# Gate vectors and norm columns of a fused adaLN, attention and gMLP kernel: from fp32 sums to float32r sums, with the columns by way of memory

## The chip, the cores and the metric

The kernel runs on one core of a Trainium2 chip. The time is that of one execution on the device, in microseconds; a result is the median of three timed runs. A profile is one further execution with the hardware profiler on. In the profile PE is the matrix engine (PEld its weight loads), DVE the vector engine, ACT the scalar engine, POOL is GpSimd, and SP issues most DMAs. Each engine works through a queue of its own in order; the engines wait for each other by semaphores.

## What is computed

The input is x (2048 tokens of 448 numbers) with a conditioning vector c. From c come six vectors of 448: `sa`, `ca`, `ga` for the attention block and `sb`, `cb`, `gb` for the second block.

```
mod = silu(c) @ w_mod                      # six vectors: sa, ca, ga, sb, cb, gb
h = layernorm(x) * (1 + ca) + sa
x = x + ga * (attention(h @ wqkv, 16 heads of 28) @ wo)
h = layernorm(x) * (1 + cb) + sb
z = gelu(h @ w_in);  z1 = z[:, :896];  z2 = layernorm(z[:, 896:])
x = x + gb * ((z1 * (w_sp @ z2 + b_sp)) @ w_out)
```

`sa, ca, sb, cb` are needed as columns (one number a partition), because they scale the transposed tokens. `ga` and `gb` are needed as rows repeated in all 128 partitions.

## The kernel before

Nearly every matmul uses float32r operands, which PE takes at full pace but with a shortened mantissa. To keep accuracy each operand is held as a high part (a float32r copy) and a low part (the rest), and the products high by high, high by low and low by high are summed: the list `STEPS` has eleven such products for one tile.

The order on each engine is that of the program's text (`manual_schedule`); the program lays it out by hand. PSUM has a ring of seven banks (`bank`), and one bank beside it. The tokens are worked on in four groups of 512 (`g`), 128 tokens a tile (`t`).

The part that the change touches is the projections, the first 90 us:

- `ln_stat` (DVE) takes mean and variance of a token tile, `ln_rs` (GpSimd) turns the variance into 1/std, `ln_norm` (DVE) writes the normalised tile `xn`, of which ACT copies the last 64 columns once more. `ln_transpose` lets PE transpose sixteen blocks into four banks; ACT scales them (`hfull`) and writes the high part of `hT[g]`, DVE the low part.
- `v_mm`/`v_tile` project V for a tile of tokens; `qk_unit` projects 128 rows of Q and K for a group. Its result is split into `qh` and `ql`, and SP stores both to `qk_scr` in memory, from where `load_head` fetches the rows of one head.
- `qk_part` splits the weights of Q and K: ACT the high part, DVE or GpSimd the low part. Kind "a" is the first 512 columns, in four parts of 128 (the last of 64) rows.
- `mod_acc` (DVE) adds up the products of `silu(c)` with a 112-row slice of `w_mod`; after four slices `acc` holds 112 partial sums for each of two vectors. `mod_bc` (L233) sums over the 112 partitions by one fp32 matmul with a matrix of ones, which gives the row in all partitions; `mod_col` (L228) uses five fp32 matmuls of one column each, and one DVE add. An fp32 matmul stands as two rows in the profile. Pair 0 (`sa`, `ca`) has a path of its own. Pair 1 is (`ga`, `sb`), pair 2 (`cb`, `gb`).

The order in the program: group 0's projections with the weight splits; `ln_next(1)`, which transposes group 1 and takes the statistics of group 2 between the low parts; the Q and K units of group 0; then the loop over g = 1 to 3: two V tiles, `ln_next(g + 1)`, two V tiles with `mod_acc` and, for g = 2, the sums of pair 1 between them, two Q and K units. For g = 3 the first head's tiles `kst` and `qst` are cleared (`pads`), `load_head(0)` and two units come first, then four V tiles and the sums of pair 2. Behind it 18 more units are interleaved with the score matmuls of the first heads (`mt`, L528), and the attention follows.

Tiles come from pools with a fixed number of buffers for a tag. In the pool `stage` the tags `qh` and `qf` have two buffers each; a tile that takes a buffer over waits for the readers of the one before, a DMA among them.

Of the kernel before, what the change touches and what calls it, by code (L numbers as in the profile page):

```python
# [8 lines left out]
F32 = mybir.dt.float32  # L9
F32R = mybir.dt.float32r  # L10
AF = mybir.ActivationFunctionType
ALU = mybir.AluOpType
# [4 lines left out]
S, D, H, DH, FH = 2048, 448, 16, 28, 896  # L17
# [11 lines left out]
STEPS = STEPS_MAIN + STEPS_Z  # L29
# [4 lines left out]
def tile_adaln_mha_gmlp(ctx, tc, x, wqkv, wo, w_in, w_spT, b_sp, w_out, cT, w_mod, out):  # L34
    nc = tc.nc
    ctx.enter_context(tc.manual_schedule())
    pe, dve, act, pool, sp = nc.tensor, nc.vector, nc.scalar, nc.gpsimd, nc.sync
# [3 lines left out]
    scr = ctx.enter_context(tc.tile_pool(name="scr", bufs=1, space=DRAM))  # L41
# [15 lines left out]
    cols = {}  # L57
# [25 lines left out]
    def sub(eng, dst, a, hi):  # L83
        eng.tensor_tensor(out=dst, in0=a, in1=hi.bitcast(F32), op=ALU.subtract)  # L84
# [25 lines left out]
    def ln_transpose(xns, full_pool, dsts, scol, bcol, engs, los=(pool,) * 4, mid=None, after=None):  # L110

        tps = []
        for c in range(4):
            tp = bank("tp")
            tps.append(tp)
            for t in range(4):
                pe.transpose(tp[:, t * 128 : (t + 1) * 128], xns[t][:, c * 128 : (c + 1) * 128], ident)  # L117
        if mid:
            mid()
        for c in (0, 2, 1, 3):  # L120
            tp = tps[c]
            f = full_pool.tile([128, 512], F32, name="hfull")
            if engs[c] is act:
                act.activation(f, tp, AF.Identity, scale=scol[:, c : c + 1], bias=bcol[:, c : c + 1])
            else:
                engs[c].tensor_scalar(
                    out=f, in0=tp, scalar1=scol[:, c : c + 1], scalar2=bcol[:, c : c + 1], op0=ALU.mult, op1=ALU.add
                )
            hi = dsts[:, c if c < 3 else 6, :]
            if engs[c] is act:  # L130
                act.activation(hi, f, AF.Copy)
            else:
                engs[c].tensor_copy(hi, f)
            if c < 3:
                sub(los[c], dsts[:, 3 + c, :], f, hi)
            else:
                sub(los[c], hi[64:128], f[64:128], hi[64:128])
            if after:
                after(c)
# [17 lines left out]
    e2 = late_e.enter_context(tc.tile_pool(name="e2", bufs=1, side="right"))  # L157

    wv = e2.tile([128, 8, D], F32R, name="wv")
    wms, xts, raws = {}, {}, {}  # L160

    def bank(name):
        return ring.tile([128, 512], F32, name=name, tag="s")
# [25 lines left out]
    def qk_part(kind, i, eng):  # L189
        weight_part(wqk, i, raws.pop((kind, i)), act, eng, False, PARTS[kind][0])  # L190
# [26 lines left out]
    accs = {}  # L217

    def mod_acc(pair, k):
        if k == 0:  # L220
            accs[pair] = e2.tile([112, 2, D], F32, name="acc")
        wm, acc = wms.pop((pair, k)), accs[pair]
        if k == 0:
            dve.tensor_scalar(out=acc, in0=wm, scalar1=silu[:, 0:1], scalar2=None, op0=ALU.mult)
        else:
            dve.scalar_tensor_tensor(out=acc, in0=wm, scalar=silu[:, k : k + 1], in1=acc, op0=ALU.mult, op1=ALU.add)

    def mod_col(nm, acc, plus1):  # L228
        pc = bank("pc")
        for c, r, e in ((0, 0, 128), (1, 0, 128), (2, 0, 128), (3, 0, 64), (3, 64, 128)):  # L230
            pe.matmul(pc[r:e, c : c + 1], acc[:, c * 128 : c * 128 + e - r], ones[:112, 0:1], start=True, stop=True)
        dve.tensor_scalar(out=cols[nm], in0=pc[:, 0:4], scalar1=plus1, scalar2=None, op0=ALU.add)

    def mod_bc(nm, acc):
        pc = bank("pc")
        pe.matmul(pc[:, :D], ones[:112, :], acc, start=True, stop=True)
        dve.tensor_copy(bcs[nm], pc[:, :D])

    mv1, xn1 = {}, {}

    def ln_stat(g, ts):
        if g not in mv1:
            mv1[g] = e1.tile([128, 4, 2], F32, name="mv"), e1.tile([128, 4], F32, name="rs")
        for t in ts:
            st = e1.tile([128, 6], F32, name="st", bufs=4)
            dve.bn_stats(out=st, in_=xts[4 * g + t])
            dve.bn_aggr(out=mv1[g][0][:, t, :], in_=st)

    def ln_rs(g, a, e):
        mv, rs = mv1[g]  # L250
        rstd_of(mv[:, a:e, 1], rs[:, a:e], e - a)
# [27 lines left out]
    def v_tile(kt):  # L279
        v_copy(*v_mm((kt,))[0])  # L280

    def qk_unit(ms, g, mid=None):
        pqs = [bank("pq") for _ in ms]
        for j, (a, b) in enumerate(STEPS):
            if mid and j in mid:
                mid[j]()
            for m, pq in zip(ms, pqs):
                pe.matmul(pq, wqk[:, b, m * 128 : (m + 1) * 128], hT[g][:, a, :], start=j == 0, stop=j == NST - 1)  # L288
        for m, pq in zip(ms, pqs):
            hi = stage.tile([128, 512], F32R, name="qh")  # L290
            lo = stage2.tile([128, 512], F32R, name="ql")
            if mid:
                f = stage.tile([128, 512], F32, name="qf")
                act.activation(f, pq, AF.Copy)
                act.activation(hi, f, AF.Copy)
                sub(pool, lo, f, hi)
            else:
                act.activation(hi, pq, AF.Copy)
                sub(dve, lo, pq, hi)
            for i, t in enumerate((hi, lo)):  # L300
                sp.dma_start(qk_scr[i][m * 128 : (m + 1) * 128, g * 512 : (g + 1) * 512], t.bitcast(F32))
# [121 lines left out]
    for i in (0, 2, 1, 3):  # L423
        load_w("b", i, sp)
    pvs = v_mm((0, 1, 3, 2), [STEPS[j] for j in (0, 1, 2, 3, 6, 4, 5, 7, 8, 9, 10)], 3)
    ln_stat(1, (0, 1))
    qk_part("a", 0, dve)
    qk_part("a", 2, dve)
    ln_stat(1, (2, 3))
    ln_rs(1, 0, 4)  # L430
    qk_part("a", 1, dve)
    qk_part("a", 3, dve)
    load_mod(1, sp)
    for a in pvs:
        v_copy(*a)
    ln_norm(1, range(4))
    qk_unit((0, 3), 0)

    def ln_next(g):

        if g + 1 < NG:
            ln_transpose(
                xn1.pop(g), e1, hT[g], cols["ca"], cols["sa"], (act,) * 4, (dve,) * 4, None,
                lambda c: ln_stat(g + 1, ((0, 2, 1, 3).index(c),)),
            )
            ln_rs(g + 1, 0, 4)
            ln_norm(g + 1, range(4))
        else:
            ln_transpose(xn1.pop(g), e1, hT[g], cols["ca"], cols["sa"], (act,) * 4, (dve,) * 4)

    ln_next(1)
    load_x(3, sp)
# [5 lines left out]
    for g in range(1, NG):  # L458
        if g == 3:
            early.close()  # L460
            stk = att.enter_context(tc.tile_pool(name="stk", bufs=1))
            kq = [[stk.tile([128, S], F32R, name=f"{n}st{i}") for n in "kq"] for i in range(3)]
            kst, qst = [a[0] for a in kq], [a[1] for a in kq]
            npool = att.enter_context(tc.tile_pool(name="npool", bufs=2))

            def pads(i, eng):

                dve.memset(kst[i][64:128, :].bitcast(F32), 0.0)
                eng.memset(qst[i][64:128, :].bitcast(F32), 0.0)
                pool.memset(kst[i][64:86, :].bitcast(F32), 1.0)  # L470

            pads(0, dve)

            def load_head(h, c0=0, c1=S):
                k, q = kst[h % 3], qst[h % 3]
                if h > 2:
                    sp.dma_start(q[84:86, :].bitcast(F32), q[86:88, :].bitcast(F32))
                for r0, i in ((0, 0), (56, 1), (28, 0)):
                    sp.dma_start(k[r0 : r0 + 28, c0:c1].bitcast(F32), qk_scr[i][D + h * DH : D + (h + 1) * DH, c0:c1])
                for r0, i in ((0, 0), (28, 1), (56, 0)):  # L480
                    sp.dma_start(q[r0 : r0 + 28, c0:c1].bitcast(F32), qk_scr[i][h * DH : (h + 1) * DH, c0:c1])

            load_head(0, 0, 1536)
            for m in (0, 3):
                qk_unit((m,), g)
            load_head(0, 1536, S)
        v_tile(4 * g)
        v_tile(4 * g + 1)
        if g == 3:
            pads(1, pool)  # L490
            pads(2, pool)
        if g + 1 < NG:
            ln_next(g + 1)
        for k in range(2):
            v_tile(4 * g + 2 + k)
            if g == 2 and k == 0:
                mod_bc("ga", accs[1][:, 0, :])
                mod_col("sb", accs[1][:, 1, :], 0.0)
            if g < 3:
                mod_acc(g, k)  # L500
        if g < 3:
            for k, m in enumerate((0, 3)):
                qk_unit((m,), g)
                mod_acc(g, 2 + k)
    mod_col("cb", accs[2][:, 0, :], 1.0)
    mod_bc("gb", accs[2][:, 1, :])
    late_e.close()


# [579 lines left out]
    acc = {}  # L1089
# [241 lines left out]
```

## Time and profile before

| | |
|---|---|
| median of three runs | 1407.74 us (1406.87 to 1410.05) |
| the profiled execution | 1407.27 us |
| its span, first to last instruction | 1405.3 us |
| granted clock of PE | 1.0 |
| bytes moved by DMA | 186.99 MB, 133 GB/s in the mean |

A row of a timeline gives start, duration (of all instructions merged into it), engine, line, operation, output and inputs, shapes and count; in brackets stands the idle time just before and what ended it. Matmuls are pipelined, so their durations overlap: the pace is read from start to start. A row "SPq" is the issue of a DMA by SP, not its transfer. A row of grouped instructions gives busy time, mean duration in ns, and idle time before.

### The profile page before, as it was taken

Reading aid. Unit: us, or ns where it says so; the run is one execution under the profiler, and the core shown is the slowest. Engines: PE = TensorE matmul, PEld = TensorE weight load, DVE = VectorE, ACT = ScalarE, POOL = GpSimd, SP = SyncE. Lnnn points to the kernel's source line nnn. Section 1 sums busy time; section 2 is a strip of 40 time slices with the busy share of each in tenths; the row PEclk is TensorE's granted clock in tenths of the full one; section 3 lists DMA queues with packets and bytes.
Section 4 is the critical chain, followed back from the end, with each engine's and each line's share of the span. In section 5 each row is a group of like instructions: output and inputs, shape, how many; then the busy total and the mean of one; then the engine's idle time right before and its main releaser. Section 6 shows DMA issues by size and latency. Waiting matters only on the chain.

```text
span 1405.3 us, 20320 instructions
## 1 busy us (share of the span) xinstructions
PE 1394.6 (99%) x7180; PEld 982.8 (70%) x7180; DVE 1011.5 (72%) x1700; ACT 787.6 (56%) x1532; POOL 286.3 (20%) x276
## 2 busy tenths in 40 slices
PE   8999999999999999999999999999999999999998
PEld 7888655555555555555555554988998888888888
DVE  7778888888888888888888860851357555768574
ACT  4623677777777777777777779263234543434211
POOL 3033312222314243313200021100132330001000
PEclk9999999999999999999999999999999999999999
DMA  8564635555455545654423001533103333445453
GB/s 256 156 176 157 190 106 175 167 161 148 162 166 162 160 163 174 180 153 155 127 68 74 22 18 33 192 121 137 55 0 107 111 113 111 144 136 162 142 170 112
DMA packets 98252, 186.99 MB, mean 133 GB/s; under 512 B 16614, under 2 KB 28006, under 8 KB 95606
## 3 DMA queue, kind: packets, MB, share of 16 engines
q1 hardware_dynamic: 95722, 181.87, 42.7%
q10 hardware_dynamic: 2430, 3.84, 0.7%
q8 instruction: 56, 0.92, 0.3%
q14 instruction: 44, 0.36, 0.1%
HBM read 130.42 MB, written 50.45 MB: 129 GB/s over the span
## 4 chain that ended last, share of the span: by engine, by line
PE 95%; DVE 2%; DMA 1%; ACT 0%; issue 0%; POOL 0%; SPq 0%; DVEq 0%; ACTq 0%; POOLq 0%
PE st_ps L559 19%; PE o_ps L574 17%; PE mt L528 17%; PE acc L1099 6%; PE acc L1100 6%; PE acc L1098 6%; PE z_ps L1024 5%; PE z_ps L910 5%; PE pq L288 4%; PE wo_ps L780 3%; PE pv L273 2%; PE y_ps L1203 2%; PE y_ps L1204 2%; PE y_ps L1202 2%; DMA wm<-in_w_mod_dram 1%; PE tp L117 1%
## 5 line engine op out<-in xcount | busy, mean ns | idle before, releaser
L533 DVE TENSOR_REDUCE pm<-mt 128x1 f32<-128x512 f32 x1024 | 631.2, 680 | 108.9 <-PE mt L528 108.8
L563 ACT ACTIVATE P<-st_ps 128x512 f32<-128x512 f32 x1024 | 513.4, 621 | 150.0 <-PE st_ps L559 149.7
L559 PE MATMUL st_ps<-qst,kst 128*128 128x512 f32 x1024 | 407.7, 409 | 0.1
L528 PE MATMUL mt<-kst,qst 128*128 128x512 f32 x1024 | 401.4, 392 | 0.0
L559 PEld LDWEIGHTS st_ps<-qst,kst 128*128 128x128 f32 x1024 | 191.0, 187 | 152.6 <-issue 82.2
L574 PE MATMUL o_ps<-P,V 128*32 128x512 f32 x2048 | 247.5, 598 | 0.0
L528 PEld LDWEIGHTS mt<-kst,qst 128*128 128x128 f32 x1024 | 192.6, 188 | 30.5 <-ACT P L563 0.7
L681 POOL TENSOR_TENSOR ws_raw<-ws_raw 128x512 f32<-128x512 f32 x80 | 103.0, 1287 | 275.6 <-DMA ws_raw<-in_w_spT_dram 275.5
L986 ACT ACTIVATE wsp_h<-raw_sp 128x512 fp32r<-128x512 f32 x112 | 70.0, 631 | 154.2 <-PE acc L1100 102.9
L84 DVE TENSOR_TENSOR wsp_l<-raw_sp,wsp_h 128x512 fp32r<-128x512 f32 x112 | 81.9, 741 | 81.3 <-ACT wsp_h L986 80.6
L574 PEld LDWEIGHTS o_ps<-P,V 128*32 128x32 f32 x2048 | 54.1, 109 | 123.3 <-issue 116.3
L1099 PE MATMUL acc<-wsp_l,heapA 128*128 128x512 f32 x224 | 87.3, 390 | 0.1
L1098 PE MATMUL acc<-wsp_h,heapA 128*128 128x512 f32 x224 | 87.3, 390 | 0.0
L1100 PE MATMUL acc<-wsp_h,heapA 128*128 128x512 f32 x224 | 87.2, 389 | 0.0
L1099 PE MATMUL acc<-wsp_l,heapB 128*128 128x512 f32 x174 | 67.7, 389 | 0.0
L1098 PE MATMUL acc<-wsp_h,heapB 128*128 128x512 f32 x174 | 67.7, 389 | 0.0
L1100 PE MATMUL acc<-wsp_h,heapB 128*128 128x512 f32 x174 | 67.7, 389 | 0.0
L288 PE MATMUL pq<-heapD,heapD 128*128 128x512 f32 x196 | 62.4, 392 | 0.0
L1028 DVE BATCH_NORM_STATS2 stz<-z 128x6 f32<-128x448 f32 x32 | 19.9, 625 | 50.4 <-ACT z L1027 30.1
L1099 PEld LDWEIGHTS acc<-wsp_l,heapA 128*128 128x128 f32 x224 | 42.0, 188 | 9.1 <-DVE wsp_l L84 0.5
L1098 PEld LDWEIGHTS acc<-wsp_h,heapA 128*128 128x128 f32 x224 | 42.0, 188 | 8.9 <-DVE cD L1104 0.3
L1100 PEld LDWEIGHTS acc<-wsp_h,heapA 128*128 128x128 f32 x224 | 42.0, 188 | 8.7
(205 smaller groups left out, 1595.0 us busy)
## 6 DMA issues: line engine op xcount, KB each, us to landing
ws_raw<-in_w_spT_dram SPq DMA_DIRECT2D x160, 256.0 KB
ws_scr<-ws_raw SPq DMA_DIRECT2D x80, 256.0 KB
raw_sp<-ws_scr SPq DMA_DIRECT2D x80, 256.0 KB
kst<-qk_scr SPq DMA_DIRECT2D x45, 224.0 KB
qst<-qk_scr SPq DMA_DIRECT2D x45, 224.0 KB
raw_sp<-in_w_spT_dram SPq DMA_DIRECT2D x32, 256.0 KB
qk_scr<-qh SPq DMA_DIRECT2D x28, 256.0 KB
qk_scr<-ql SPq DMA_DIRECT2D x28, 256.0 KB
```

Source lines behind the costliest of these rows:

```text
L84: eng.tensor_tensor(out=dst, in0=a, in1=hi.bitcast(F32), op=ALU.subtract)
L288: pe.matmul(pq, wqk[:, b, m * 128 : (m + 1) * 128], hT[g][:, a, :], start=j == 0, stop=j == NST - 1)
L528: pe.matmul(mt, qst[h % 3][:, t * 128 : (t + 1) * 128], kst[h % 3][:, kb * 512 : (kb + 1) * 512], start=True, stop=True)
L533: dve.tensor_reduce(out=pms[h][:, t, kb : kb + 1], in_=mt, axis=AX.X, op=ALU.max)
L559: pe.matmul(st, kst[h % 3][:, kt * 128 : (kt + 1) * 128], qst[h % 3][:, qb * 512 : (qb + 1) * 512], start=True, stop=True)
L563: act.activation(p, st, AF.Exp, scale=SCALE)
L574: pe.matmul(otile[h][32 * qb : 32 * qb + 32, :], V[:, kt, h, :], ptiles.pop((u, qb)), start=kt == 0, stop=kt == NT - 1)
L681: pool.tensor_tensor(out=a, in0=a, in1=b, op=SUMS[i // 16][2])
L910: pe.matmul(ps_t, w1[:, b, f * 128 : (f + 1) * 128], h2T[g][:, a, :], start=j == 0, stop=j == NST - 1)
L1098: pe.matmul(acc[i], zh, hi, start=st == 0, stop=False)
L1099: pe.matmul(acc[i], zh, lo, start=False, stop=False)
L1100: pe.matmul(acc[i], zl, hi, start=False, stop=st == 7)
```

## The change

1. Pairs 1 and 2: `mod_split` makes a float32r high part (ACT) and a low part (GpSimd) of each vector's partial sums, in buffers of the tags `qf` and `qh`. `mod_sum` sums both over the partitions by two float32r matmuls with a float32r matrix of ones. `mod_bc` copies the result. `mod_col` takes one partition's row, adds the constant, and SP stores it to memory and fetches it back as columns in three DMAs.
2. `mod_split(1)` stands within `ln_next(3)`, `mod_split(2)` behind the first V tile of g = 3. The sums of pair 1 move one V tile later. In g = 2 the four `mod_acc` move back by a place or two: the first behind the sums, the last two behind the last unit.
3. Group 1: all four statistics in one go, before the low weights of kind "a"; the low parts of parts 1 and 3 go to GpSimd and their splits ahead of those of parts 0 and 2. The first pair of Q and K units takes the products with high weights first (`HI_FIRST`).
4. `ln_next` asks for 1/std after two tiles and again after four, instead of once for all four.

```diff
+    ones_r = e2.tile([112, 128], F32R, name="ones_r")
+    dve.memset(ones_r.bitcast(F32), 1.0)
...
-    def mod_col(nm, acc, plus1):
+    def mod_split(pair):
+        acc = accs.pop(pair)
+        accs[pair] = []
+        for part in range(2):
+            h, l = (stage.tile([128, 512], F32R, name=n, tag=t)[0:112, :D] for n, t in (("acc_h", "qf"), ("acc_l", "qh")))
+            act.activation(h, acc[:, part, :], AF.Copy)
+            sub(pool, l, acc[:, part, :], h)
+            accs[pair].append((h, l))
+
+    def mod_sum(pair, part):
         pc = bank("pc")
-        for c, r, e in ((0, 0, 128), (1, 0, 128), (2, 0, 128), (3, 0, 64), (3, 64, 128)):
-            pe.matmul(pc[r:e, c : c + 1], acc[:, c * 128 : c * 128 + e - r], ones[:112, 0:1], start=True, stop=True)
-        dve.tensor_scalar(out=cols[nm], in0=pc[:, 0:4], scalar1=plus1, scalar2=None, op0=ALU.add)
-
-    def mod_bc(nm, acc):
-        pc = bank("pc")
-        pe.matmul(pc[:, :D], ones[:112, :], acc, start=True, stop=True)
-        dve.tensor_copy(bcs[nm], pc[:, :D])
+        for i, a in enumerate(accs[pair][part]):
+            pe.matmul(pc[:, :D], ones_r, a, start=i == 0, stop=i == 1)
+        return pc[:, :D]
+
+    def mod_bc(nm, pair, part):
+        dve.tensor_copy(bcs[nm], mod_sum(pair, part))
+
+    def mod_col(nm, pair, part, plus1):
+        row, dst = e2.tile([1, D], F32, name="row"), scr.tile([D], F32, name=f"{nm}_scr")
+        dve.tensor_scalar(out=row, in0=mod_sum(pair, part)[0:1], scalar1=plus1, scalar2=None, op0=ALU.add)
+        sp.dma_start(dst.rearrange("(o n) -> o n", o=1), row)
+        for r, e, c in ((0, 128, slice(0, 3)), (0, 64, slice(3, 4)), (64, 128, slice(3, 4))):
+            src = dst[0:384] if e - r == 128 else dst[384:D]
+            sp.dma_start(cols[nm][r:e, c], src.rearrange("(c p) -> p c", p=e - r))
...
+    HI_FIRST = [p for p in STEPS if p[1] in (0, 1, 2, 6)] + [p for p in STEPS if p[1] in (3, 4, 5, 7)]
+    def qk_unit(ms, g, mid=None, order=STEPS):
...
-    ln_stat(1, (0, 1))
+    qk_part("a", 1, pool)
+    qk_part("a", 3, pool)
+    ln_stat(1, (0, 1, 2, 3))
+    ln_rs(1, 0, 4)
     qk_part("a", 0, dve)
     qk_part("a", 2, dve)
-    ln_stat(1, (2, 3))
-    ln_rs(1, 0, 4)
-    qk_part("a", 1, dve)
-    qk_part("a", 3, dve)
...
-    qk_unit((0, 3), 0)
+    qk_unit((0, 3), 0, order=HI_FIRST)
+
+    def ln_step(g, t):
+        ln_stat(g, (t,))
+        if t % 2:
+            ln_rs(g, t - 1, t + 1)
...
-                lambda c: ln_stat(g + 1, ((0, 2, 1, 3).index(c),)),
+                lambda c: ln_step(g + 1, (0, 2, 1, 3).index(c)),
             )
-            ln_rs(g + 1, 0, 4)
             ln_norm(g + 1, range(4))
         else:
-            ln_transpose(xn1.pop(g), e1, hT[g], cols["ca"], cols["sa"], (act,) * 4, (dve,) * 4)
+            ln_transpose(
+                xn1.pop(g), e1, hT[g], cols["ca"], cols["sa"], (act,) * 4, (dve,) * 4, None, lambda c: c == 2 and mod_split(1)
+            )
...
         v_tile(4 * g)
+        if g == 3:
+            mod_split(2)
         v_tile(4 * g + 1)
...
-            if g == 2 and k == 0:
-                mod_bc("ga", accs[1][:, 0, :])
-                mod_col("sb", accs[1][:, 1, :], 0.0)
-            if g < 3:
-                mod_acc(g, k)
+            if g == 2 and k == 1:
+                mod_bc("ga", 1, 0)
+                mod_col("sb", 1, 1, 0.0)
+            if g == 1 or g == 2 and k == 1:
+                mod_acc(g, k if g == 1 else 0)
         if g < 3:
             for k, m in enumerate((0, 3)):
                 qk_unit((m,), g)
-                mod_acc(g, 2 + k)
-    mod_col("cb", accs[2][:, 0, :], 1.0)
-    mod_bc("gb", accs[2][:, 1, :])
+                mod_acc(g, 3 - g + k)
+            if g == 2:
+                mod_acc(g, 3)
+    mod_col("cb", 2, 0, 1.0)
+    mod_bc("gb", 2, 1)
```

More of the change, by code (lines that the diff above doesn't have):

```diff
@@ L280, in v_tile @@
         v_copy(*v_mm((kt,))[0])
-    def qk_unit(ms, g, mid=None):
+    HI_FIRST = [p for p in STEPS if p[1] in (0, 1, 2, 6)] + [p for p in STEPS if p[1] in (3, 4, 5, 7)]
+    def qk_unit(ms, g, mid=None, order=STEPS):
         pqs = [bank("pq") for _ in ms]
-        for j, (a, b) in enumerate(STEPS):
+        for j, (a, b) in enumerate(order):
             if mid and j in mid:
```

## The prediction

> **What bounds the kernel now.** I read the page first, then the waits of PE over the first 140 us, then PE's timeline there; the queries of DVE, GpSimd (POOL), ACT and SP come at the terms that need them.
>
> ```profile
> span 1405.3 us, 20320 instructions
> PE 1394.6 (99%) x7180; PEld 982.8 (70%) x7180; DVE 1011.5 (72%) x1700; ACT 787.6 (56%) x1532; POOL 286.3 (20%) x276
> ...
> PE 95%; DVE 2%; DMA 1%; ACT 0%; issue 0%; POOL 0%; SPq 0%; DVEq 0%; ACTq 0%; POOLq 0%
> ```
>
> PE is busy for 99% of the span and holds 95% of the chain that ends last. So a microsecond taken from PE's own queue, or from a gap in it, shortens the run; work on other engines counts only where PE comes to wait for it. The profiled execution took 1407.27 us, 1.97 more than its span; the median of the three timed runs is 1407.74, 0.47 above it. My sum is made against 1407.27.
>
> The change lies in the first 90 us. PE's timeline there (start, duration, count; the stage runs in PE's order, so a start minus the start before it is what a step cost):
>
> ```profile
> 31.57 2.89 PE L117 MATMUL tp<-ident,xn 128*128 128x128 f32 x16
> 34.22 0.93 PE L288 MATMUL pq<-heapD,heapD 128*128 128x512 f32 x3
> ...
> 43.78 1.90 PE L117 MATMUL tp<-ident,xn 128*128 128x128 f32 x12
> 45.98 0.66 PE L117 MATMUL tp<-ident,xn 128*128 128x128 f32 x4 [0.30 <-DVE ql L84]
> 46.58 4.75 PE L273 MATMUL pv<-wv,heapD 128*128 128x448 f32 x22
> ...
> 56.21 4.65 PE L273 MATMUL pv<-wv,heapD 128*128 128x448 f32 x22
> 60.69 1.91 PE L117 MATMUL tp<-ident,xn 128*128 128x128 f32 x16
> 62.35 2.50 PE L273 MATMUL pv<-wv,heapD 128*128 128x448 f32 x11
> 64.69 0.92 PE L236 MATMUL pc<-acc,ones 112*128 112x448 f32 x2
> ...
> 66.31 2.50 PE L273 MATMUL pv<-wv,heapD 128*128 128x448 f32 x11
> 68.65 0.86 PE L288 MATMUL pq<-heapD,heapD 128*128 128x512 f32 x3
> ...
> 87.60 0.94 PE L231 MATMUL pc<-ones,acc 112*128 112x1 f32 x10
> ...
> 89.56 0.39 PE L528 MATMUL mt<-kst,qst 128*128 128x512 f32 x1
> ```
>
> The busy figure hides the stalls: sixteen transposes take 2.65 us from start to next start for group 1 (34.22 - 31.57), 2.80 for group 2 (46.58 - 43.78), and 1.66 for group 3 (62.35 - 60.69). The third is the free pace, so 0.99 and 1.14 us are waiting.
>
> **The change, part by part.**
>
> *The sums on PE.* A float32r matmul of 448 columns starts every (60.69 - 56.21) / 22 = 0.204 us. The first pair of fp32 sums and columns costs 66.31 - 64.69 = 1.62 us, and the eleven matmuls behind it take 2.34 instead of 11 x 0.204 = 2.24, so 1.72. The second pair ends one matmul (0.23) before the mt at 89.56: 89.33 - 87.60 = 1.73. Together 3.45. In their place stand eight float32r matmuls, 8 x 0.204 = 1.63. PE's own work: -1.82, that is -0.91 at each of the two places.
>
> *Statistics of group 1, two low weights on GpSimd, high products first.* What held the transposes back:
>
> ```profile
> 24.62 0.63 DVE L246 BATCH_NORM_STATS2 st<-xg 128x6 f32<-128x448 f32 x1
> ...
> 28.95 0.59 POOL L107 TENSOR_SCALAR rs<-mv 128x4 f32<-128x4 f32 x1 [5.64 <-DVE mv L247]
> ...
> 30.99 1.78 DVE L257 TENSOR_SCALAR xn<-xg,mv,rs 128x448 f32<-128x448 f32 x4 [0.94 <-POOL rs L108]
> ...
> 42.65 1.78 DVE L257 TENSOR_SCALAR xn<-xg,mv,rs 128x448 f32<-128x448 f32 x4 [1.47 <-POOL rs L108]
> 45.24 1.29 DVE L84 TENSOR_TENSOR ql<-pq,qh 128x512 fp32r<-128x512 f32 x2 [0.81 <-ACT qh L298]
> ```
>
> The four statistics begin at 24.62 and end before 28.95 with two low weights between them. Those two, some 0.6 us each (like the pair of ql in 1.29), leave this place, so rs starts 1.2 earlier and xn at 29.8. PE reaches the transposes at 31.57 as before, and the last xn is then done. The 0.99 goes. The lows of parts 1 and 3 now come from GpSimd, those of 0 and 2 from DVE behind the statistics, at about 28.9; the order with high products first asks for them after 14 of 22 matmuls, 3.2 us into the unit. They are in time, so I cost them at nothing; without that reordering PE would ask for part 0's at the third step and wait about 1 us.
>
> For group 2 the rstd comes in two halves, so two of the four xn no longer sit out the 1.47 us for GpSimd: xn ends some 1.1 earlier, besides the 1.1 that the whole chain has moved. The ql that frees the fourth transpose's bank (45.98 waits for it) ended at 45.24 + 0.69 = 45.9 and ends by 43.7; PE, at the transposes by 43.78 - 0.99 = 42.8, needs it after three quarters of 1.66, at 44.0. The 1.14 goes too, with 0.3 to spare; what is late next is the second ql, at 46.5 - 2.2 = 44.3 for a need at 44.45. Bounds: 0 to 2.13 for both, taken 2.13, as both chains come out ahead.
>
> *The splits (new waits).* Each pair needs two ACT copies and two GpSimd subtracts. For pair 1 they start well before PE asks; ACT carries the 1 us, which only group 3's projections, far behind, wait for. Pair 2 is different. Its low halves use the buffers of tag qh, of which there are two, and both have just been filled for head rows that SP stores to memory. In the built program the first subtract waits for the store of unit m = 0 of group 3 to land, and the second waits for PE's matmul that reads the first (it gets the same buffer). Behind these on GpSimd stand four memsets, for which head 1's loads and the next ql wait, with room; PE itself waits for the results.
>
> ```profile
> 74.48 0.69 DVE L84 TENSOR_TENSOR ql<-pq,qh 128x512 fp32r<-128x512 f32 x1 [0.74 <-ACT qh L298]
> 75.09 1.15 DVE L226 SCALAR_TENSOR_TENSOR acc<-wm,silu,acc 112x896 f32<-112x896 f32 x1
> 76.72 1.76 DVE L468 MEMSET kst<- 64x2048 f32 x1 [0.49 <-DVE acc L226]
> ...
> 78.77 1.81 POOL L470 MEMSET kst<- 22x2048 f32 x1 [22.05 <-DVE kst L468]
> ```
>
> ```profile
> 74.48 0.32 SPq L301 DMA_DIRECT2D qk_scr<-qh  x1
> ...
> 77.04 0.37 SPq L479 DMA_DIRECT2D kst<-qk_scr  x1
> ...
> 82.67 0.37 SPq L301 DMA_DIRECT2D qk_scr<-qh  x1
> ...
> 83.61 0.38 SPq L301 DMA_DIRECT2D qk_scr<-qh  x1
> ...
> 89.11 0.94 SPq L479 DMA_DIRECT2D kst<-qk_scr  x2
> ```
>
> ```profile
> L84 POOL TENSOR_TENSOR wv<-raw,wv 64x448 fp32r<-64x448 f32 x1 | 1.6, 1593 | 0.0
> ...
> L84 POOL TENSOR_TENSOR wv<-raw,wv 128x448 fp32r<-128x448 f32 x1 | 1.2, 1154 | 0.0
> ```
>
> Up to there PE is 0.99 + 1.14 + 0.91 = 3.04 early: it asks for the first sum at 87.60 - 3.04 = 84.56 and for its low half 0.2 later, 84.76. The store starts later than that shift: DVE now has two accumulates behind the last ql where it had one (1.07 more), so kst's memset is at 76.72 + 1.07 - 3.04 = 74.75, GpSimd's (2.05 behind) ends at 78.6, and the store, 2.09 after that end, is issued at 80.7. An unhindered store lands within 77.04 - 74.48 = 2.56; the third of this burst took until 89.11, 5.5 us, and the first cannot have landed after it, 6.44. It is nearer the third, behind the same loads: I take 4.8, so 85.5. The subtract takes 1.15 (the 128x448 row; 1.59 is the upper end), and PE goes on at 86.7: **1.95** lost (0 to 4.0). Then matmul (0.37: 4.65 - 21 x 0.204), subtract 1.15 and two hand-overs of 0.05, less the 0.41 of two matmuls that PE would need anyway: **1.2** lost (0.9 to 1.7).
>
> The two GpSimd rows differ by 0.44 though the longer one has half the rows; it ran beside DVE's subtracts. The Trainium skill (GPSIMD Engine Reference, section 8, Key points) says that GpSimd shares its SBUF interfaces with VectorE and is in contention with DVE instructions that read two SBUF inputs. The trace agrees; by that rule the subtracts of pair 1, which stand beside such work, take the longer price and those of pair 2 the shorter, and the sum stays within the bounds above.
>
> *The columns through memory.* DVE adds one row instead of four columns. SP gets four DMAs a time, and the second waits on SP for the first to land. sb's are needed by the second norm alone, 800 us on. cb's stand ahead of the loads of head 1 and of all stores of the interleaved units behind; see the first rival. I cost them at nothing: cover is the slack counted there.
>
> *Sum:* -1.82 - 2.13 + 1.95 + 1.2 = -0.8; 1407.27 - 0.8 = **1406.5**. After 90 us the order of work is the same and PE is dense, so the shift should reach the end.
>
> **Rivals.**
>
> *Slower: SP's round trip for cb makes PE wait in the interleaved units.* Place:
>
> ```profile
> 94.45 0.34 SPq L301 DMA_DIRECT2D qk_scr<-qh  x1
> ```
>
> ```profile
> 103.03 0.63 ACT L295 ACTIVATE qh<-qf 128x512 fp32r<-128x512 f32 x1 [1.96 <-DMA qk_scr<-qh]
> 104.10 0.60 ACT L294 ACTIVATE qf<-pq 128x512 f32<-128x512 f32 x1 [0.43 <-PE pq L288]
> ```
>
> ```profile
> 107.47 0.39 PE L288 MATMUL pq<-heapD,heapD 128*128 128x512 f32 x1
> ```
>
> ACT already waits for the first unit's store, issued at 94.45 behind head 1's loads, until 103.03. The qf at 104.10 frees the bank of the unit that starts at 107.47. Slack: 107.47 - 104.70, and 0.44 of idle ACT: 3.2 us. New on SP: one landing plus three issues of 0.4. SP itself stands 1.2 earlier against PE: the loads ahead went out at 89.11 for PE's 89.33, and go out at 80.7 + 0.94 + 5.5 = 87.1 for 88.5. So it decides at a landing of 3.2 us; beyond it PE loses one for one.
>
> ```profile
> 846.77 0.33 SPq L591 DMA_DIRECT2D r_scr<-rt  x1
> 848.19 0.58 SPq L597 DMA_DIRECT2D rb<-r_scr  x1
> ```
>
> A small write landed in 1.42 us on an idle queue; in this burst 5.5 is the upper end. If both the write and the columns take 5.5 (2.5 of the second lie beside head 1's issues), PE loses 5.5 + 1.2 - 1.2 - 3.2 + 3.0 = 5.3: **1411.8**. For it: six loads stand in the queue ahead. Against: at 3 us nothing happens. The Trainium skill (DMA: Bandwidth & Descriptors, Rules for kernel authors) has a non-contiguous last dimension lowered to one descriptor per element, here 384 of four bytes; no row of before has such a transfer, and it speaks for this rival.
>
> *Faster: the store lands early*, as the unhindered 2.56 does. Then only the second wait is left: -1.82 - 2.13 + 1.2 = -2.75: **1404.5**. Against it: 5.5 for the third store.
>
> *The transposes still wait* (it doesn't do what it says): the margins of 0.3 and 0.15 us fail, or xn is held by ACT. Then -1.82 + 3.15 = +1.3: **1408.6**. For it: ql waits for ACT at 45.24. Against: xn is earlier by more than the margin needs.
>
> **How the numbers follow.** Forecast 0.55 (own range 1405.0 to 1408.0), early store 0.20, transposes still wait 0.13, SP's round trip 0.12. A measurement of this kernel tells about 0.2% from no change, 2.8 us around 1407.74: 1404.9 to 1410.6. Faster: the early store and the forecast's lower edge, 0.23; slower: the round trip and a little of the transposes' case, 0.14; same 0.63. The range runs from the early store to past the case of the transposes, 1404.2 to 1409.5, and leaves out the round trip and single tails.
>
> **What would show it.** Right: transposes of groups 1 and 2 at 1.66 start to start; eight pc matmuls at 0.2; PE waiting for GpSimd's acc_l twice in the second sums, about 2 and 1.2 us, the first subtract released by a DMA of qh; no wait of pq for ACT near 107. Wrong: no such wait, or a wait at the fifth or sixth unit, or transposes over 2 us.

## The result, and the profile after

The changed kernel takes 1411.93 us (median of nine runs, 1410.11 to 1416.38), the kernel before 1407.92 beside it (nine runs, 1406.59 to 1410.05): a ratio of 1.003, interval 1.0019 to 1.004. It is 4.0 us slower; the forecast was 1406.5, and 1411.93 lies above the range of 1404.2 to 1409.5. The profiled execution took 1411.94 us.

The page of the changed kernel, its first lines and the shares of the chain that ended last:

```profile
span 1410.0 us, 20323 instructions
...
PE 1395.1 (99%) x7164; PEld 984.3 (70%) x7164; DVE 1015.0 (72%) x1699; ACT 789.1 (56%) x1536; POOL 297.3 (21%) x286
...
PE 97%; DVE 1%; DMA 1%; ACT 0%; POOL 0%; SPq 0%; issue 0%; POOLq 0%; DVEq 0%; ACTq 0%
```

PE is still the bound and its busy time is nearly what it was (1394.6 before), though the span grew by 4.7. So the loss is waiting, or matmuls that take longer. The waits of PE (us in all, times, longest) in the changed kernel, but for one of 5.0 at the very start that both kernels have:

```profile
PE pc L244 <- POOL acc_l L84: 3.3, 2, 2.2
PE pv L292 <- DVE heapD L84: 1.7, 3, 0.9
PE tp L343 <- DVE xn L276: 1.3, 1, 1.3
```

and, of the second of these kinds, in the kernel before:

```profile
PE pv L273 <- DVE heapD L84: 0.2, 1, 0.2
```

The first row was forecast. The second was not: V's matmuls of group 0 wait for DVE's low parts of group 0, which the change does not touch. PE's timeline of the changed kernel at that place and at the transposes of groups 1 and 2:

```profile
17.61 5.14 PE L292 MATMUL pv<-wv,heapD 128*128 128x448 f32 x24
22.91 1.89 PE L292 MATMUL pv<-wv,heapD 128*128 128x448 f32 x8 [0.17 <-DVE heapD L84]
25.72 1.08 PE L292 MATMUL pv<-wv,heapD 128*128 128x448 f32 x4 [0.92 <-DVE heapD L84]
27.41 3.06 PE L292 MATMUL pv<-wv,heapD 128*128 128x448 f32 x8 [0.61 <-DVE heapD L84]
30.27 3.35 PE L310 MATMUL pq<-heapD,heapD 128*128 128x512 f32 x12
...
35.73 1.91 PE L117 MATMUL tp<-ident,xn 128*128 128x128 f32 x16
37.40 0.94 PE L310 MATMUL pq<-heapD,heapD 128*128 128x512 f32 x3
...
46.97 1.91 PE L117 MATMUL tp<-ident,xn 128*128 128x128 f32 x16
48.63 1.67 PE L292 MATMUL pv<-wv,heapD 128*128 128x448 f32 x7
```

Sixteen transposes take 1.67 (37.40 - 35.73) and 1.66 us: both stalls are gone, as forecast (the last row is cut off at the end of the view). But 30.27 - 17.61 = 12.66 us pass from the first V matmul to the first of Q and K, where the kernel before took 9.46 (26.54 - 17.08 in its timeline). The eight matmuls at 27.41 take 2.86 where 8 x 0.204 is 1.63, with no wait between them. DVE's two kinds of low parts in that stretch, in the changed kernel (busy, mean ns):

```profile
L84 DVE TENSOR_TENSOR heapD<-hfull,heapD 128x512 fp32r<-128x512 f32 x2 | 3.8, 1936 | 0.0
L84 DVE TENSOR_TENSOR heapD<-hfull,heapD 64x512 fp32r<-64x512 f32 x1 | 1.7, 1662 | 0.0
```

and in the kernel before:

```profile
L84 DVE TENSOR_TENSOR heapD<-hfull,heapD 128x512 fp32r<-128x512 f32 x2 | 2.5, 1301 | 0.0
...
L84 DVE TENSOR_TENSOR heapD<-hfull,heapD 64x512 fp32r<-64x512 f32 x1 | 0.7, 690 | 0.0
```

The same three instructions take 5.5 us instead of 3.3. Beside them GpSimd now works, in the changed kernel:

```profile
21.14 2.72 POOL L84 TENSOR_TENSOR wv<-raw,wv 128x448 fp32r<-128x448 f32 x2
23.83 1.29 POOL L84 TENSOR_TENSOR heapF<-raw,heapD 128x512 fp32r<-128x512 f32 x1
25.07 1.74 POOL L84 TENSOR_TENSOR heapF<-raw,heapF 64x512 fp32r<-64x512 f32 x1
```

The last two are the low weights that the change gave to GpSimd. The second sums, on PE and on GpSimd:

```profile
88.70 0.37 PE L244 MATMUL pc<-acc_h,ones_r 112*128 112x448 f32 x1
91.24 0.47 PE L244 MATMUL pc<-acc_l,ones_r 112*128 112x448 f32 x1 [2.17 <-POOL acc_l L84]
91.55 0.37 PE L244 MATMUL pc<-acc_h,ones_r 112*128 112x448 f32 x1
93.04 0.74 PE L244 MATMUL pc<-acc_l,ones_r 112*128 112x448 f32 x1 [1.12 <-POOL acc_l L84]
93.58 0.63 PE L310 MATMUL pq<-heapD,heapD 128*128 128x512 f32 x1
94.00 0.63 PE L559 MATMUL mt<-kst,qst 128*128 128x512 f32 x1
```

```profile
90.06 1.13 POOL L84 TENSOR_TENSOR acc_l<-acc,acc_h 112x448 fp32r<-112x448 f32 x1 [7.15 <-DMA qk_scr<-qh]
91.86 1.13 POOL L84 TENSOR_TENSOR acc_l<-acc,acc_h 112x448 fp32r<-112x448 f32 x1 [0.67 <-PE pc L244]
```

Start to start, less one matmul of 0.204, the waits cost 2.34 (91.24 - 88.70) and 1.29 us (93.04 - 91.55), the first released by a store of qh, the second by PE's read. But the matmul behind them starts 0.42 us before its successor (94.00 - 93.58), not 0.23. The granted clock says why (us of the stretch, PE busy, clock, DMA share, GB/s; changed kernel):

```profile
27.00:28.00 1.00, 0.58 (x2) 0.89 0.78 241
28.00:29.00 1.00, 1.00 (x4) 0.50 1.01 251
...
31.00:32.00 1.00, 1.00 (x5) 0.90 0.03 8
...
92.00:93.00 1.00, 0.00 (x0) 0.82 0.16 33
93.00:94.00 1.00, 0.96 (x2) 0.50 0.44 111
...
96.00:97.00 1.00, 1.00 (x5) 0.98 0.00 0
```

PE has half its clock twice for some 3.3 us, and counts as busy meanwhile: in windows of 0.25 us the clock is 0.50 from 27.8 to 31.1 us, beginning behind the first gap, and from 92.6 to 96.0, beginning within the last wait of the second sums. The page's mean of the whole run is 0.998, which doesn't say where it falls. Among the nine timed runs the mean goes with the time: 1410.1 to 1411.0 us at 0.999, 1411.7 to 1412.7 at 0.998, 1416.4 at 0.992. One stretch of 3.3 us at half clock is 0.0012 of a mean over 1410 us, so some runs have more such stretches than others; where those lie is not on record.

All profiles of this study by stage, in us, from the starts of PE's rows (and of ACT's first `nf`, the transposed maxima of head 0): A up to the first V matmul; B to the first Q and K matmul; C to the transposes of group 1; D to the second sums; E to `nf`; F to the end.

| kernel | A | B | C | D | E | F |
|---|---|---|---|---|---|---|
| before | 17.08 | 9.46 | 5.03 | 56.03 | 58.08 | 1259.6 |
| changed | 17.61 | 12.66 | 5.46 | 52.97 | 62.81 | 1258.5 |
| e1 before + two GpSimd subtracts | 19.45 | 11.55 | 5.21 | 56.01 | 58.08 | 1259.7 |
| e2 changed, low weights behind | 17.58 | 10.60 | 4.99 | 52.97 | 62.63 | 1259.7 |
| e3 changed, own lows | 17.43 | 11.53 | 5.04 | 53.01 | 62.74 | 1260.5 |
| e4 both edits | 18.19 | 10.61 | 5.04 | 52.97 | 62.76 | 1260.7 |
| e5 own lows, kept | 17.22 | 10.27 | 5.03 | 53.02 | 58.92 | 1261.0 |
| e6 both, kept | 17.88 | 9.45 | 5.00 | 52.98 | 58.91 | 1261.4 |
| e7 as e2, PE filled | 17.29 | 9.47 | 5.04 | 52.97 | 60.92 | 1259.7 |
| e8 points 1 and 2 alone | 17.04 | 9.45 | 5.04 | 55.10 | 62.93 | 1260.8 |
| e9 as e6, columns on ACT | 18.30 | 9.22 | 5.00 | 52.97 | 57.15 | 1261.2 |
| e10 points 3 and 4 alone | 17.59 | 11.52 | 5.04 | 54.06 | 58.08 | 1261.3 |
| e11 changed, again | 17.49 | 11.51 | 5.05 | 53.01 | 62.94 | 1260.0 |
| e12 before, again | 18.21 | 9.46 | 5.04 | 55.99 | 58.12 | 1259.7 |

The first two rows differ by +0.53 + 3.20 + 0.43 - 3.06 + 4.73 - 1.13 = +4.7, the growth of the span.

### The profile page after: what moved, and what is told of

The parts are those of the page before. It is cut to its first block, busy times and chain, and to the rows that moved or that the text cites. A ratio compares the mean times of both kernels' runs of the same rounds, so it can differ in the third digit from the quotient of the medians.

```text
span 1410.0 us, 20323 instructions
## 1 busy us (share of the span) xinstructions
PE 1395.1 (99%) x7164; PEld 984.3 (70%) x7164; DVE 1015.0 (72%) x1699; ACT 789.1 (56%) x1536; POOL 297.3 (21%) x286
## 4 chain that ended last, share of the span: by engine, by line
PE 97%; DVE 1%; DMA 1%; ACT 0%; POOL 0%; SPq 0%; issue 0%; POOLq 0%; DVEq 0%; ACTq 0%
PE st_ps L590 19%; PE o_ps L605 17%; PE mt L559 17%; PE acc L1130 6%; PE acc L1129 6%; PE acc L1131 6%; PE z_ps L1055 5%; PE z_ps L941 5%; PE pq L310 5%; PE wo_ps L811 3%; PE pv L292 2%; PE y_ps L1234 2%; PE y_ps L1235 2%; PE y_ps L1233 2%; PE tp L117 1%; DMA wm<-in_w_mod_dram 1%
```

## The experiments

Theory A: GpSimd's low weights hold off DVE's low parts, for which PE waits (stage B); the splits of pair 2 wait for two buffers (stage E); and behind a gap PE's clock is halved. The rivals are named in the expectations. A ratio is that to the kernel before, run beside the experiments (medians 1409.59 for e1 to e4, 1409.57 for e5 to e8, 1408.58 for e9 to e11).

### e1: two more GpSimd subtracts in the kernel before

```diff
     wv_lo(3, pool)
...
+    sub(pool, wqk[:, 4, 0:512], fs[0], hT[0][:, 0, :])
+    sub(pool, wqk[0:64, 4, 0:512], fs[0][0:64], hT[0][0:64, 0, :])
     pvs = v_mm((0, 1, 3, 2), ...
```

> The kernel before with two GpSimd subtracts added behind its last low part of wv (128x512 and 64x512, read from hfull and group 0's high part, written to a place that DVE overwrites later); nothing waits for them but that later write. Theory A (GpSimd's two-input subtracts hold off DVE's low parts of group 0, PE waits for these, and its clock is halved for some 3 us after the gap): DVE's last two low parts of group 0 take 2 to 5 us together instead of 2.3, PE needs 10.1 to 12.7 us from its first V matmul to its first Q and K matmul instead of 9.46, time 1408.5 to 1411. Rival B (the loss there comes from the order of the high splits and late loads of the raw weights): low parts as before, 9.46 us, 1407.9.

1412.46 us, ratio 1.0021 (1.0012 to 1.003), 2.9 us slower. DVE and GpSimd in it:

```profile
23.72 5.49 DVE L84 TENSOR_TENSOR heapD<-hfull,heapD 128x512 fp32r<-128x512 f32 x3
```

```profile
25.66 3.00 POOL L84 TENSOR_TENSOR heapF<-hfull,heapD 128x512 fp32r<-128x512 f32 x2
```

Work that nobody waits for makes the three low parts last 5.49 us, as in the changed kernel, and stage B 2.09 longer. The high splits and the loads of the raw weights are those of the kernel before here, so rival B falls. The clock stayed whole behind this gap; the long A of this profile (19.45) has a halved clock of its own, from 13.7 to 17.1, behind a wait of 1.9 us at the start.

### e2: the low weights behind DVE's low parts

```diff
+    gate_t = e1.tile([128, 1], F32, name="gate_t", bufs=1)
+    pool.tensor_copy(gate_t[64:128], hT[0][64:128, 6, 0:1].bitcast(F32))
     pvs = v_mm((0, 1, 3, 2), ...
```

> The changed kernel with one tiny GpSimd copy ahead of the two low weights; it reads group 0's last low part, so that the two subtracts start only when DVE has finished its own. Theory A: DVE's three low parts take 3.3 us again instead of 5.5, PE's first V matmul to first Q and K matmul 9.5 us instead of 12.7, no half clock there; 1/std of group 1 is up to 0.5 us later behind the moved subtracts, which the transposes may show; 1411.9 - 3.2 + 0.3 = 1409.0. Rival B (load order): 12.7 us and 1411.9 stay.

1411.36 us, ratio 1.0014 (1.0005 to 1.0022). DVE and GpSimd:

```profile
21.84 3.24 DVE L84 TENSOR_TENSOR heapD<-hfull,heapD 128x512 fp32r<-128x512 f32 x3
```

```profile
25.22 0.19 POOL L448 COPY gate_t<-heapD 64x1 f32<-64x1 f32 x1 [1.41 <-DVE heapD L84]
25.48 1.30 POOL L84 TENSOR_TENSOR heapF<-raw,heapD 128x512 fp32r<-128x512 f32 x1
26.73 1.29 POOL L84 TENSOR_TENSOR heapF<-raw,heapF 64x512 fp32r<-64x512 f32 x1
```

The low parts are back at 3.24, no wait of V's matmuls is left, and stages C and D lose nothing by the delay. GpSimd gains as well: its last low weight takes 1.29 us here and 1.74 beside DVE's low parts. B is 10.60 and not 9.5: in this run the transposes of the first tokens waited 2.5 us at the start (1.3 in the changed kernel), and the clock was halved from about 18 to 21.5, 5 us behind the end of that wait; that the wait caused it is not shown. With the same edit B is 9.47 in e7 and 9.45 in e6.

### e3 and e4: own places for pair 2's low halves

```diff
-            h, l = (stage.tile([128, 512], F32R, name=n, tag=t)[0:112, :D] for n, t in (("acc_h", "qf"), ("acc_l", "qh")))
+            h = stage.tile([128, 512], F32R, name="acc_h", tag="qf")[0:112, :D]
...
+            if pair == 2:
+                l = qst[2][0:112, part * D : (part + 1) * D]
+            else:
+                l = stage.tile([128, 512], F32R, name="acc_l", tag="qh")[0:112, :D]
```

> The changed kernel with the low halves of pair 2 in a place of their own (in head 2's qst, which is not in use yet) instead of the two buffers of qh, so that neither a store nor PE's read is waited for. Theory A (the two waits and a half clock for 3.4 us behind them): both waits for acc_l go, the granted clock stays at 1.0 there, from the first of the second sums to the end of the first interleaved unit 4.9 us are saved, 1407.0. Rival C (the waits alone cost; the slow matmuls behind them have another cause, such as head 1's loads or stores): 3.4 saved, 1408.5, and the slow matmuls stay. Rival D (GpSimd is late for another reason): 1411.9.

> The changed kernel with both edits: the tiny copy that lets the two low weights start behind DVE's low parts, and places of their own for the low halves of pair 2. Theory A: what is left of the change is the shorter sums (-1.8) and the freed transposes (-2.1, less up to 0.5): 1407.9 - 3.6 = 1404.3. If the two losses had a common cause, or one moved the other, the sum of the two single savings would not come: 1406 or more.

e3: 1412.09, ratio 1.0016 (1.0007 to 1.0026). e4: 1410.32, 1.0006 (0.9997 to 1.0015). Both missed: the place was badly chosen. GpSimd clears rows 64 to 127 of that tile ahead of the sums, so rows 64 to 111 of the low halves are lost from the sums, and PE waited 1.95 us in each for the clearing; E stayed at 62.7, with four late score matmuls in it (1.76, see e6). One thing can be kept: a single gap of 1.95 us is followed by a halved clock too. PE and its clock in e4:

```profile
89.14 0.47 PE L249 MATMUL pc<-qst,ones_r 112*128 112x448 f32 x1 [1.95 <-POOL qst L503]
```

```profile
90.00:92.00 2.00, 2.00 (x8) 0.58 0.29 79
92.00:94.00 2.00, 2.00 (x7) 0.57 0.33 94
```

### e5 and e6: the clearing behind the sums

```diff
-                eng.memset(qst[i][64:128, :].bitcast(F32), 0.0)
+                if i < 2:
+                    eng.memset(qst[i][64:128, :].bitcast(F32), 0.0)
...
     mod_bc("gb", 2, 1)
+    pool.memset(qst[2][64:128, :].bitcast(F32), 0.0)
```

> As the third run, but the clearing of head 2's qst on GpSimd is moved behind the sums of pair 2, since in the third run PE waited 1.95 us for that clearing, which overwrote the low halves. Ratio to before of the changed kernel was 1.003 (+4.0 us). Theory A (waits for a store and for a read, then half clock): GpSimd's two subtracts stand together ahead of 85 us, no wait for them, granted clock 1.0 behind the sums; -4.9 us, ratio 0.9995, about the time before. Rival C (the slow matmuls behind have a cause of their own): the clock row stays at 0.5, -3.4, ratio 1.0005. Rival D (GpSimd is late whatever the place): 1.003.

> The tiny GpSimd copy ahead of the two low weights, and the low halves of pair 2 in places of their own, cleared behind the sums. Theory A: neither loss is left; what remains is the shorter sums (-1.8) and the freed transposes (-2.1): ratio 0.9973, 3.9 us under the time before. Rival E (time given back elsewhere, at the start or in the attention, which the sum by stages does not see): within 0.1% of before.

e5: 1409.04, ratio 0.9992 (0.9983 to 1.0001). e6: 1406.67, ratio 0.9981 (0.9972 to 0.999). PE's second sums in e5:

```profile
85.54 0.37 PE L249 MATMUL pc<-acc_h,ones_r 112*128 112x448 f32 x1
85.75 0.36 PE L249 MATMUL pc<-qst,ones_r 112*128 112x448 f32 x1
...
86.36 0.39 PE L315 MATMUL pq<-heapD,heapD 128*128 128x512 f32 x1
```

Both waits and the half clock are gone, and e6 without both losses is faster than the kernel before. But E is 58.91, where 58.08 - 0.93 = 57.15 was to be had: 1.76 us came back elsewhere. DVE in e6, at the ninth and tenth of the interleaved units:

```profile
116.18 0.69 DVE L573 TENSOR_REDUCE pm<-mt 128x1 f32<-128x512 f32 x1 [0.60 <-PE mt L568]
117.46 0.69 DVE L573 TENSOR_REDUCE pm<-mt 128x1 f32<-128x512 f32 x1 [0.59 <-PE mt L568]
```

DVE waits 0.59 for the next mt where 0.22 is the rule: there four mt come 0.37 late, and the two units take 4.55 and 4.02 us instead of 3.40, 1.77 more. In the built program those mt get the PSUM bank of the mt one or two before, so that each waits for DVE's reading of it. The changed kernel has one such mt, at 124.32 (its units there lie 3.79 apart instead of 3.40: 0.39).

e5 shows more of the mechanism of stage B. There the raw weights came a little later, GpSimd's first low weight did not start until 0.1 us after wv's, and DVE's second low part went ahead of it: 1.63 us, as before; only the third was held, 1.67 instead of 0.69, and B is 10.27.

### e7: PE filled while it would wait

```diff
         for i, a in enumerate(accs[pair][part]):
+            if pair == 2 and i == 1:
+                for _ in range((10, 5)[part]):
+                    pe.matmul(fill[:, :D], hT[3][:, 0, 0:128], wv[:, 0, :], start=True, stop=True)
```

> The tiny copy ahead of the low weights as in the second run, and in the second sums ten and five float32r matmuls that nobody reads, between the high and the low matmul, so that PE works while it would wait for GpSimd. Theory A (a gap costs itself and then a halved clock): PE goes on at the same time as in the second run, but the granted clock stays at 1.0, so the first interleaved unit takes 3.6 us instead of 4.9: 1.2 to 1.6 us less than the second run, ratio 1.0004 instead of 1.0014. Rival C (the matmuls behind the wait are slow for what runs beside them): unit of 4.9 us, ratio 1.0014.

1408.61 us, ratio 0.9993 (0.9984 to 1.0002). PE, and its clock behind the sums:

```profile
84.77 0.37 PE L249 MATMUL pc<-acc_h,ones_r 112*128 112x448 f32 x1
84.98 2.21 PE L248 MATMUL fill<-wv,heapD 128*128 128x448 f32 x10
87.15 0.47 PE L249 MATMUL pc<-acc_l,ones_r 112*128 112x448 f32 x1
```

```profile
88.00:90.00 2.00, 1.87 (x10) 1.00 0.35 100
90.00:92.00 2.00, 2.00 (x10) 1.00 0.22 73
```

The delay is nearly the same, the clock stays whole. From the first of the second sums to ACT's read of the first interleaved unit it takes 8.45 us, against 9.73 in e2, 9.96 in the changed kernel and 4.71 in e5. The waits cost 3.74, and the half clock 1.28 against e2, from which e7 differs by the unread matmuls and their bank alone, or 1.51 against the changed kernel, whose first wait is 0.16 longer. So matmuls that do nothing gain 1.3 us, within the forecast of 1.2 to 1.6; rival C falls. The median is 2.75 us under that of e2, more than this: e7 has no late mt either (0.39 in e2), and the mean clock is 1.000 in all eleven runs of e7 and 0.995 to 0.999 in those of e2, most of which so have more than one slow stretch.

### e8 and e10: each half of the change alone

e8 is the changed kernel with the lines of before for group 1's statistics, the low weights, the order of the first units and `ln_next`; e10 the kernel before with the lines of the change for these.

> Points 1 and 2 of the change alone (float32r sums, columns through memory, splits, order of mod_acc); statistics and low weights as before. Theory A: -1.8 for PE's work, +2.0 and +1.2 for the waits, +1.6 for a half clock behind them: +3.0, ratio 1.0021; the transposes of groups 1 and 2 stall as before (2.65 and 2.80 us for sixteen). If the columns' round trip through memory had a price of its own (rival), PE would also wait in the fifth or sixth interleaved unit, and the ratio would be 1.004 or more.

> Points 3 and 4 of the change alone (statistics of group 1 in one go, two low weights on GpSimd, high products first, 1/std in halves), with the fp32 sums, columns by matmul and the order of mod_acc of before. Theory A: transposes of groups 1 and 2 at 1.66 us, -2.1; the gap in group 0's V matmuls +2.1, and up to +1.6 more where the clock is halved behind it: 0 to +1.6, ratio 1.000 to 1.001. If the low weights cost nothing, as the prediction had it: ratio 0.9985.

e8: 1414.55, ratio 1.0033 (1.0021 to 1.0046). e10: 1408.19, ratio 0.9996 (0.9987 to 1.0004). In e8 D is shorter by 0.93 and E longer by 4.85, 3.9 in all where 3.0 was forecast. Its interval reaches past the rival's 1.004, but no fifth or sixth unit waits in the trace; one mt is late (0.39), and the rest lies in the waits and the half clock. In e10 D is shorter by 1.97 and B longer by 2.06: its gain and its loss cancel, and 0.9985, the ratio if the low weights cost nothing, lies just outside the interval. The clock stayed whole behind the gap in e10.

### e9: the columns by ACT's queue

```diff
-        sp.dma_start(dst.rearrange("(o n) -> o n", o=1), row)
+        q = act if pair == 2 else sp
+        q.dma_start(dst.rearrange("(o n) -> o n", o=1), row)
...
-            sp.dma_start(cols[nm][r:e, c], src.rearrange("(c p) -> p c", p=e - r))
+            q.dma_start(cols[nm][r:e, c], src.rearrange("(c p) -> p c", p=e - r))
```

> As the sixth run (both edits), and the four DMAs of cb are issued by ACT instead of SP, so that SP's stores of the interleaved units stand no longer behind the row's landing. In the sixth run ACT waited 6.9 us for a store of qh at the third unit, and in the ninth and tenth units four mt matmuls came 0.37 us late each: there the mt that follows gets the bank of the mt just before it and waits for DVE to read it. In the changed kernel's program one such wait is seen, in this one's order of banks none. Theory F (cb's round trip on SP holds the stores, and through them the order in which banks come free): no late mt, ACT's wait about 2 us, 1.5 us less than the sixth run, ratio 0.9970. Rival G (PE being earlier is enough for that): late mt stay, ratio 0.9981.

1405.51 us, ratio 0.9981 (0.9972 to 0.9989). DVE at the units where e6 was late, and ACT:

```profile
116.01 0.69 DVE L574 TENSOR_REDUCE pm<-mt 128x1 f32<-128x512 f32 x1 [0.21 <-PE mt L569]
```

```profile
103.63 0.63 ACT L323 ACTIVATE qh<-qf 128x512 fp32r<-128x512 f32 x1 [5.59 <-DMA qk_scr<-qh]
```

No mt is late there, and E is 57.15: the whole gain of the shorter sums. ACT's wait for the store is still 5.6 us, so it is not the store's time in the run that makes mt late, as Theory F had it, but the order of banks in the built program, which this edit changes as well: in e6 four mt get the bank of the mt just before them, in e9 none does. The ratio doesn't show the 1.7 us against e6: F is long in both, and the intervals are as wide as the effect.

### e11 and e12: both kernels once more

> The changed kernel as it is, on the chip of these runs, for comparison with them: ratio 1.003 as before. In its profile the gap of group 0 and the two waits of pair 2 must be there again (1.7 us in three pieces, 2.2 and 1.1 us); the clock behind the second was halved in every profile with those waits so far, behind the first in one of three.

> The kernel before once more, for a second profile of it. From PE's first V matmul to its first Q and K matmul 9.46 us, from there to the transposes of group 1 5.03, to the second sums 56.0, to the first nf 58.1, as in the first profile: these stages hold no DMA that PE waits for. If the start (17.08 us until the first V matmul) and the part behind the first nf (1259.6 us) differ by 0.5 us and by 1 to 2 us from the first profile, then the like differences among the kernels of this study are of the run and not of the change. If both come out the same within 0.1 us, the differences are of the kernels and want a cause.

e11: 1414.08, ratio 1.0043 (1.003 to 1.0056); its other four runs, at mean clocks of 0.994 to 0.997, are 1.1 to 3.2 us longer than the profiled one at 0.999. Its gaps are those of the first profile (1.7; 2.1 and 1.1), the clock is halved behind the second alone, and so B is 11.51 and C 5.05: the gap costs 2.05, a half clock behind it 1.15 + 0.41 more.

e12 (one run, 1408.36): B to E lie within 0.04 us of the first profile. A differs by 1.13, so the start is a matter of the run, and with it the +0.53 of the changed kernel. F is the same within 0.1 us, which by what was expected would make the other differences in F a matter of the kernels; but the changed kernel's own two profiles are 1.5 apart there. The difference is spread over the heads of the attention, and its cause stays open.

## Why the prediction was wrong

| term | forecast | measured | from |
|---|---|---|---|
| sums on PE, both places | -1.82 | -1.86 | D in e8 (-0.93), E in e9 (-0.93) |
| transposes of groups 1 and 2 | -2.13 | -2.13 | D: -3.06 + 0.93; e10 alone: -1.97 |
| two waits of pair 2 | +3.15 | +3.74 | e7 against e5 (3.63 from the changed kernel's own rows) |
| low weights on GpSimd | 0 | +2.05 | B in e1, e10, e11 |
| half clock behind pair 2's waits | not there | +1.51 | changed against e7 (1.28 from e2 against e7) |
| half clock behind group 0's gap | not there | 0 or +1.56 | changed against e11 |
| columns through memory | 0 | 0 | no wait for them in any trace |
| order of PSUM banks | not there | +0.39 | one late mt; 1.76 in e6 |
| sum | -0.8 | +3.7, or +5.3 | |

**The step that failed** is "They are in time, so I cost them at nothing". The two low weights were in time for PE, but they cost 2.05 us. What they do to another engine while they run was not asked. The trace of before held the answer: DVE's two 128x512 low parts had a mean of 1301 ns there, one 0.97 and one 1.63 us, and the long one ran beside GpSimd's wv:

```profile
L84 DVE TENSOR_TENSOR heapD<-hfull,heapD 128x512 fp32r<-128x512 f32 x1 | 1.0, 972 | 0.0
...
L84 DVE TENSOR_TENSOR heapD<-hfull,heapD 128x512 fp32r<-128x512 f32 x1 | 1.6, 1630 | 0.0
```

The prediction priced that contention for GpSimd (1.154 against 1.593) and not for DVE, whose low parts PE was waiting for already (0.2 us). By itself this step would have left the time inside the range (about 1408.5); with the second omission, below (1.51 more), it does not.

How the two engines share the memory fits the Trainium skill (SBUF — State Buffer, Terms and Who interferes with whom): a DVE instruction with two SBUF inputs contends with a GpSimd instruction that reads SBUF (the memory on the chip), and the one that has the shared interface blocks the other for its whole length. The traces agree: in the changed kernel GpSimd's first low weight ends at 25.12 (23.83 + 1.29), and V's next matmul, released by DVE's second low part, starts 0.60 later, about the length of one unhindered low part (0.67); in e5 DVE came first, and B lost 0.8 us, not 2.05.

**The second omission** is the clock, which cost 1.51 us behind pair 2's waits and in one of two profiles of the changed kernel 1.56 more behind group 0's gap. A wait of PE was priced by its length, as if PE went on at full pace behind it. The Trainium skill (TensorE: Matmul & The Clock Gate, What's actually happening) says that the clock falls to half after an idle window of about 3.4 us and returns after a busy one of that length, and that the windows run freely. The length of the slow stretch agrees (3.3 us); the condition does not: 1.95 us in one piece were enough in e3 and e4, and 1.7 in three pieces in one of five profiles (the changed kernel; not in e1, e3, e10, e11). What decides between these is not shown.

**What was right:** PE's work, both transposes, and both waits with their releasers; the first was estimated at 1.95 and came to 2.34 (the store took 5.0 us to land, not 4.8, and was issued 0.2 later against PE), the second at 1.2 and came to 1.29.

**The rivals.** SP's round trip gave the right total (1411.8) by a wrong mechanism: the row landed in 1.5 us, under the 3.2 from which it was to decide, and no fifth or sixth unit waited. The order of banks (0.39) changed with points 1 and 2: one mt is late in e8 and none in e10. That the columns alone changed it is not shown. The store did not land early (5.0 us), and the transposes did not wait.

## What to carry to other kernels

Work given to an idle engine is not free while it runs: ask which instructions of another engine read two operands from that memory at that time, as DVE's subtracts did beside GpSimd's here, and whether the bound waits for them; a mean that mixes a short and a long instance of one operation is the trace's hint. A wait of PE costs its length and, from about 2 us on in these traces, can cost 1.3 to 1.6 us more by a halved clock; read the clock by the microsecond, not from the run's mean. The parts of the change were worth 4.0 us, and with the two losses mended (e6, e9) the kernel is 0.19% faster than before (some 2.7 us; intervals 0.9972 to 0.999). Where the rest went is open in part: late mt in e6, a longer F in both.

## What was not expected of the hardware

- In the second sums PE's clock was halved every time, behind one gap of 1.95 us (e3, e4) or behind gaps of 2.0 to 2.2 and 1.1 us (changed, e2, e8, e11). Behind the gap at the start it was halved at once in e1 (1.9 us), 5 us later in e2 and e4 (2.5 and 2.9), and not in e3, e6 and e7 (2.3 to 2.7).
- Fifteen matmuls that nobody reads, in the two gaps, kept it whole (e7): 1.3 us against e2.
- One order of PSUM banks against another, with the same instructions on PE, went with 1.76 us in stage E (e6 against e9).
